# Attention and SoLU MLP on one core: a search for the order of issue that replays each candidate, one DMA moved to another queue, and another order of the first loads

## The chip, the cores and the metric

The kernel runs on one core of one Trainium2 chip. A core has a matrix engine (TensorE, PE in the profile; its weight loads are shown apart as PEld), VectorE (DVE), ScalarE (ACT), GpSimd (POOL) and SyncE (SP), each with its own instruction queue that it works off in order, and 16 DMA engines that they share. "SPq" and "ACTq" in the profile are the queues through which SyncE and ScalarE issue DMAs. The metric is the device time of one execution in microseconds (us); lower is better. The kernel before took 397.25 us in the median of 3 runs (396.76 to 397.73).

## What is computed

Block-sparse attention over 4 batches, 8 heads, 768 positions and 64 channels a head, and then a SoLU MLP over the 3072 tokens of 512 channels (inner width 1024). Each query sees the keys nearer than 16 positions and, for each block of 32 positions, one summary key (the maximum over the block) with one summary value (the mean over the block).

```python
k_sum = k.reshape(B, H, nb, block, D).max(axis=3)
v_sum = v.reshape(B, H, nb, block, D).mean(axis=3)
scores_l = where(|i - j| < 16, scale * q @ k.T, -1e9)
scores_s = scale * einsum('bhsd,bhnd->bhsn', q, k_sum) + log(block)
a = softmax(concat([scores_l, scores_s]))
x = a @ concat([v, v_sum])            # then (B*S, H*D)
h = x @ w_in
solu = h * softmax(h)
out = ((solu - mean) / sqrt(var + 1e-6) * g_ln) @ w_out
```

## The kernel before, in words

**Tiles and stages.** Queries are handled in groups of 256 positions, three groups to a batch, so 12 groups; a group is handled in two halves of four heads. A query tile of 64 positions sees a window of 96 keys and the 24 block maxima, 120 columns in all. For each half group there is a matmul step for the scores (`scores`, line 578; masked on VectorE at line 597, exponentiated on ScalarE at line 605, normalised at lines 610 to 615), a transpose (`values_turn`, line 633) and the product with the values (`values`, line 672), whose result is copied out of the accumulator as a rounded high part (`xh`, line 677) and a rest (`xl`, line 678). The value tile `vt` of a group holds 96 window rows in its partitions and, in partitions 96 to 119, the 24 block means, which a small DMA (`load_v2`, line 541) copies from the tile `vsum`.

The MLP works on 24 tiles of 128 tokens: `first` (line 697: 24 matmuls of 512 columns for both halves, then maxima, exponentials, products and sums on VectorE, ScalarE and GpSimd), `turn` (transpose, and split into a high part and a rest) and `second` (line 775: 24 matmuls, then a scaled copy at line 780 and the store at line 785). The weights come as 64-bit words and are split on the chip into a rounded high part and a rest (`rounded`, lines 359 to 389; `split_w_in`, `split_w_out`), some seven operations a piece of 512 KB, on ScalarE, VectorE and, for some, GpSimd. There are 8 pieces of `w_in` and 8 of `w_out`. All of that splitting falls into the first 100 us.

**Block means.** Batch 0's are summed by matmuls over rows loaded for that purpose (`mean_values_first`, line 459) and land in `vsum`. Batch 1's are summed likewise at line 472, copied to a tile `vs` on ScalarE, and from there four small DMAs on ScalarE's queue (line 485) put them into `vsum`. There is one buffer for `vsum`, so batch 1's may be written only when the last DMA that reads batch 0's has landed; that last one is the third group's `load_v2`. Batches 2 and 3 are summed on GpSimd (`add_rows`, line 501) and one matmul (line 516).

**What sets the order.** The code does not issue instructions as it goes. Each step is recorded by `op` (line 107) with the engines that could do it, a cost on each, what it reads and writes, and a number that is its place in the program (`prio`). Then `Plan.issue` (line 141) works out an order: `due` is the least place of any matrix-engine operation that depends on the step, or for SyncE's DMAs their own place. `order` (line 172) simulates: at each step it takes, over all engines, the operation that could begin first, and among those that could begin at the same time the one with the least `due`; an operation that several engines can do goes to the one where it would end first, with a surcharge. DMAs share one modelled channel (270 GB/s to 6.9 us, 410 after), begin at the earliest 1 us after issue, and land 0.6 us after their bytes until `LATE`, and 2.0 us after them from then on. `issue` tries the program order once and 63 others, in each of which every `due` has a random number with a spread of 3 added; it keeps the order whose last matrix-engine operation ends first in the simulation. Then the instructions are issued in that order, each engine getting its own in turn. The order is fixed when the program is built. On the chip each instruction waits for what it needs, so an engine whose next instruction is not ready stands still, whatever stands behind it.

While it issues, `issue` follows the simulated time of the matrix engine, and where that has nothing to do before 80 us, `keep_up` (line 243) puts in filler matmuls of zeros (line 900) of 0.22 us each.

**First loads.** `LOADS` (line 47) is a string of letters, one for each of the first 20 DMAs of SyncE: k for the keys of one head pair (410 KB), q for half of the first group's queries (262 KB), w for a piece of `w_in` (524 KB), r for rows for the means (524 KB each, 3 of them), v for the first group's values (1049 KB), Q and V for the second group's queries (524 KB) and values (1049 KB). It gives the places from which the search starts.

**The means of a group.** `load_v2(b, g)` (line 538) waits for `vsum` and for `vt`'s own load, since both write `vt`. For batch 0 it is issued by ScalarE, for the others by SyncE; the first group of batch 0 takes its means straight from `vsum` (line 664) and has no such DMA.

## Time and profile before

| what | us |
|---|---|
| median of 3 runs | 397.25 |
| the profiled execution's own time | 397.45 |
| its span, first to last instruction | 395.7 |
| matrix engine busy (PE) | 386.6 |
| weight loads (PEld) | 298.3 |
| VectorE (DVE) | 275.4 |
| ScalarE (ACT) | 248.7 |
| GpSimd (POOL) | 97.9 |
| last matmul ends | 392.65 |
| bytes moved | 49.24 MB |

In the rows of a timeline stand the start, the length, the engine, the line in the kernel, the operation with what it writes and reads, and how many instructions were merged; in brackets, the idle time of the engine just before and what ended it. In groups of instructions stand the busy time in all, the mean duration in ns, and the idle time before them. A row of busy times by stretch gives, for each engine, busy us and the number of instructions, then the granted clock of the matrix engine, the share of time that the DMA engines were busy, and GB/s. In the chain of waits a row is a start, a length and what that time was spent on; "issue" is time in which the engine waited for nothing that the profile shows.

### The profile page before, as it was taken

What the parts mean: (1) busy time and instruction counts of PE and PEld (TensorE: products, weight loads), DVE (VectorE), ACT (ScalarE), POOL (GpSimd) and SP (SyncE); (2) the same over time, 40 slices, a digit from 0 to 9 for tenths busy, and PEclk for the clock granted to TensorE, in tenths of its full rate; (3) what the DMA queues carried; (4) which work ended last, traced back from release to release, by engine and by line L of the source; (5) the groups of instructions that cost most, each with busy time, mean ns of one, the idle gap of its engine ahead of it and who ended that gap; (6) DMA issues with size and microseconds to landing.
All of it is one profiled execution on the core that took longest, in us unless ns stands there. A gap on an engine that the chain in (4) does not pass through costs nothing.

```text
span 395.7 us, 9677 instructions
## 1 busy us (share of the span) xinstructions
PE 386.6 (98%) x3697; PEld 298.3 (75%) x3703; DVE 275.4 (70%) x884; ACT 248.7 (63%) x746; POOL 97.9 (25%) x245
## 2 busy tenths in 40 slices
PE   8999998999999999999999999999999999999996
PEld 3436766677878888878888888878888887878776
DVE  4999998999789866577767657657657654554330
ACT  3889686999798756658558466468466463533411
POOL 4224010416837221236220121221021021101100
PEclk9999999999999999999999999999999999999999
DMA  7999992136277320463330410430310000000011
GB/s 287 411 410 369 409 329 78 56 113 185 70 248 208 113 103 0 141 175 104 123 112 2 150 66 27 156 73 28 108 48 27 2 28 27 16 12 28 27 55 53
DMA packets 14994, 49.24 MB, mean 124 GB/s; under 512 B 1836, under 2 KB 2092, under 8 KB 13412
## 3 DMA queue, kind: packets, MB, share of 16 engines
q1 hardware_dynamic: 11084, 41.89, 30.8%
q10 hardware_dynamic: 3864, 6.74, 4.7%
q8 instruction: 29, 0.48, 0.5%
q14 instruction: 17, 0.14, 0.1%
HBM read 40.11 MB, written 6.29 MB: 117 GB/s over the span
## 4 chain that ended last, share of the span: by engine, by line
PE 85%; DMA 6%; ACT 3%; DVE 2%; issue 1%; ACTq 1%; SPq 1%; DVEq 0%
PE o L775 35%; PE h L697 30%; PE x L672 6%; PE s L578 5%; PE t L633 3%; PE lt L633 3%; DMA st_v<-in_vr 3%; DMA raw<-in_w_in 2%; DMA vt<-vsum 2%; PE vs_ps L459 1%; PE x L900 1%; ACT he L712 1%; DVE he L720 1%; ACT at L281 1%; PE x L664 1%
## 5 line engine op out<-in xcount | busy, mean ns | idle before, releaser
L775 PE MATMUL o<-w,lh 128*128 128x512 f32 (+1 forms) x400 | 128.0, 390 | 0.1
L697 PE MATMUL h<-w,xh 128*128 128x512 f32 x384 | 127.0, 398 | 0.4 <-DVE he L720 0.4
L605 ACT ACTIVATE e<-e,nm 128x120 f32<-128x120 f32 x192 | 73.1, 385 | 25.0 <-DVE nm L597 25.0
L775 PEld LDWEIGHTS o<-w,lh 128*128 128x128 f32 x400 | 74.1, 188 | 18.5 <-issue 2.4
L697 PEld LDWEIGHTS h<-w,xh 128*128 128x128 f32 x384 | 72.1, 188 | 18.9 <-ACT e L605 0.8
L775 PE MATMUL o<-w,ll 128*128 128x512 f32 (+1 forms) x200 | 76.9, 384 | 0.0
L697 PE MATMUL h<-w,xl 128*128 128x512 f32 x192 | 75.6, 394 | 0.0
L707 DVE TENSOR_REDUCE hm<-h 128x1 f32<-128x512 f32 x48 | 32.6, 686 | 42.7 <-PE h L697 42.7
L281 ACT COPY at<-t 120x512 f32<-120x512 f32 x46 | 24.8, 587 | 46.1 <-PE t L633 45.6
L775 PEld LDWEIGHTS o<-w,ll 128*128 128x128 f32 x200 | 37.6, 188 | 6.6
L697 PEld LDWEIGHTS h<-w,xl 128*128 128x128 f32 x192 | 36.1, 188 | 7.5
L597 DVE CUSTOM_DVE_ANT_0 e<-s,mask 128x120 f32<-128x120 f32 x192 | 40.6, 276 | 1.3 <-PE s L578 1.3
L712 ACT ACTIVATE he<-h,hm 128x512 f32<-128x512 f32 x48 | 32.8, 697 | 9.4 <-DVE hm L709 9.4
L605 ACT ACTIVATION_READ_ACCUMULATOR e<-e,nm 128x1 f32 x192 | 36.5, 190 | 0.0
L760 DVE TENSOR_TENSOR ll<-lt,lh 128x512 fp32r<-128x512 f32 x48 | 31.9, 682 | 6.0 <-ACT lh L281 5.8
L739 POOL TENSOR_SCALAR ss<-ss 128x1 f32<-128x1 f32 x24 | 7.1, 297 | 115.0 <-ACT sq L735 114.9
L720 DVE SCALAR_TENSOR_TENSOR he<-h,hz,he 128x512 f32<-128x512 f32 x48 | 34.1, 746 | 0.4
L672 PE MATMUL x<-at,vt 120*64 120x64 f32 (+1 forms) x768 | 28.3, 225 | 1.5 <-ACT at L281 1.5
L672 PEld LDWEIGHTS x<-at,vt 120*64 120x64 f32 (+1 forms) x768 | 24.6, 138 | 6.3 <-ACT at L281 2.8
L288 DVE TENSOR_TENSOR e<-e,z 128x960 f32<-128x960 f32 x23 | 26.6, 1156 | 0.5
L281 ACT CAST lh<-lt 128x512 fp32r<-128x512 f32 x33 | 18.6, 596 | 12.9 <-PE lt L633 10.0
L735 ACT ACTIVATE sq<-he 128x1024 bf16<-128x1024 f32 x24 | 25.2, 1050 | 0.2
(94 smaller groups left out, 499.6 us busy)
## 6 DMA issues: line engine op xcount, KB each, us to landing
vt<-in_v SPq DMA_DIRECT2D x12, 1024.0 KB, 5.4
kraw<-in_k SPq DMA_DIRECT2D x16, 400.0 KB, 9.1
out<-os ACTq DMA_DIRECT2D x23, 256.0 KB, 2.0
qt<-in_q SPq DMA_DIRECT2D x11, 512.0 KB, 5.5
raw<-in_w_in SPq DMA_DIRECT2D x8, 512.0 KB, 10.7
raw<-in_w_out SPq DMA_DIRECT2D x8, 512.0 KB, 9.5
st_v<-in_vr SPq DMA_DIRECT2D x6, 512.0 KB, 12.5
st_v<-in_vb SPq DMA_DIRECT2D x8, 384.0 KB, 3.3
```

Of the source, the lines that this page charges most:

```text
L281: by = {act: lambda: nc.scalar.copy(out=to(), in_=of()), dve: lambda: nc.vector.tensor_copy(out=to(), in_=of()), pool: lambda: nc.gpsimd.t ...
L288: by = {dve: lambda: nc.vector.tensor_tensor(out=to(), in0=a(), in1=b(), op=kind), pool: lambda: nc.gpsimd.tensor_tensor(out=to(), in0=a() ...
L597: nc.vector.tensor_tensor_reduce(out=e.ap[:, n, :], in0=sc.ap[:, j, (2 * i + up) * KC:(2 * i + up + 1) * KC], in1=mask[:, mi, :], scale=-S ...
L605: nc.scalar.activation(out=e.ap[:, n, :], in_=e.ap[:, n, :], func=AF.Exp, bias=nm.ap[:, n:n + 1], scale=-1.0, accum_out=z.ap[:, n:n + 1])
L672: nc.tensor.matmul(xp()[j * D:(j + 1) * D, i, qs], vs.ap[:k, u, cs], at.ap[:k, u % 2, n[j] + u // 2, :], start=not apart, stop=not apart o ...
L697: nc.tensor.matmul(hp.ap, a.ap[:, c, ts], w.ap[:, i], start=(c == 0 and n == 0), stop=(c == NKC - 1 and n == 2))
L707: op(dve, 0.6, lambda i=i, hp=hp: nc.vector.tensor_reduce(out=nms.ap[:, i:i + 1], in_=hp.ap, op=ALU.max, axis=AX.X, negate=True), r=[hp], ...
L712: op(act, 0.71, lambda i=i, hp=hp: nc.scalar.activation(out=part(i), in_=hp.ap, func=AF.Exp, bias=nm.ap, accum_out=zs.ap[:, i:i + 1]), r=[ ...
L720: op(dve, 0.67, lambda i=i, hp=hp: nc.vector.scalar_tensor_tensor(out=part(i), in0=hp.ap, scalar=zs.ap[:, 0:1], in1=part(i), op0=ALU.mult, ...
L735: op(act, 1.13, lambda: nc.scalar.activation(out=sq.ap, in_=e.ap, func=AF.Square, accum_out=ss.ap), r=[e], w=[sq, ss])
L760: op(dve, 0.6, lambda part=part, r=r: nc.vector.tensor_tensor(out=part(lo), in0=tp.ap[:, r], in1=part(hi).bitcast(F32), op=ALU.subtract), ...
L775: nc.tensor.matmul(o.ap[:, cols], a.ap[:, f, :], w.ap[:, i, cols], start=(f == 0 and n == 0), stop=(f == NFC - 1 and n == 2))
```

## The change

Four things are changed. The search tries 800 orders instead of 64: the program order, 15 in which every `due` gets a random number with a spread of 10 added, and then 784 in each of which about 2% of the steps get another such number on top of the best found so far. A new function `replay` scores an order: it keeps the order and the choice of engines, and goes through it again with durations of all engines but the matrix engine between 1.2% shorter and 4.8% longer, and with landings after `LATE` later by a random time of 1.5 us in the mean. An order's score is the sum over six such replays of the end of the last matrix-engine operation plus half the mean of all their ends; the lowest score is kept. In the simulation, `LATE` is 30 instead of 50 us, and landings after it take 2.5 instead of 2.0 us. The third group's means of batch 0 are issued by SyncE instead of ScalarE. The string of the first loads is another.

```diff
-LOADS = "wwkwqkkkqwwwrrrwwvQV"
+LOADS = "wwkqkkkwqwwrwrrvQwwV"
...
-    LATE = 50.0
+    LATE = 30.0
...
-    TRIES, NOISE = 64, 3.0
+    TRIES, NOISE = 800, 10.0
+    FIRST, FEW = 16, 0.02
+    PLAYS, JITTER, LAND = 6, 0.06, 1.5
...
-        due, best = [o.due for o in self.ops], None
-        for seed in range(self.TRIES):
-            noise = random.Random(seed)
-            for o, x in zip(self.ops, due):
-                o.due = x + (noise.gauss(0.0, self.NOISE) if seed else 0.0)
+        due, best, rnd = [o.due for o in self.ops], None, random.Random(0)
+        for i in range(self.TRIES):
+
+            noise = [x + (rnd.gauss(0.0, self.NOISE) if i < self.FIRST or rnd.random() < self.FEW else 0.0) * (i > 0)
+                     for x in (best[3] if i >= self.FIRST else [0.0] * len(due))]
+            for o, x, n in zip(self.ops, due, noise):
+                o.due = x + n
             order = self.order()
             if order:
-                end = max(o.end for o in order if "pe" in o.can)
-                if best is None or end < best[0]:
-                    best = end, order, [(o.start, o.end, o.engine, o.cost, o.fn) for o in self.ops]
-        _, order, kept = best
+                kept = [(o.start, o.end, o.engine, o.cost, o.fn) for o in self.ops]
+                end = sum(self.replay(order, random.Random(k)) for k in range(self.PLAYS))
+                if best is None or end <= best[0]:
+                    best = end, order, kept, noise
+        _, order, kept, _ = best
...
+    def replay(self, order, rnd):
+
+        free, end, held, dma, last, total, n = {}, {}, 0.0, 0.0, 0.0, 0.0, 0
+        for o in order:
+            e = o.engine
+            t = max([free.get(e, self.START)] + [end[d] + (0.0 if d.engine == e == "pe" else self.SYNC) for d in o.deps])
+            x = o.can[e][0] * (1 if e == "pe" else 1.0 + self.JITTER * (rnd.random() - 0.2))
+            other = free.get("pool", 0.0) if e == "dve" and o.port else held if e == "pool" else 0.0
+            x = t + x * (2 if e == "pe" and t < self.COLD else 1) + max(other - t, 0.0)
+            free[e] = end[o] = x
+            if e == "dve" and o.port:
+                held = x
+            if o.nbytes:
+                dma = max(dma, x + 1.0) + o.nbytes / (self.RATE if dma > self.COLD else self.SLOW) * 1e-3
+                end[o] = dma + (0.6 if dma < self.LATE else 2.5) + rnd.expovariate(1.0) * self.LAND * (dma > self.LATE)
+            if e == "pe":
+                last, total, n = max(last, x), total + x, n + 1
+        return last + 0.5 * total / n
...
-                o.end = dma + (0.6 if dma < self.LATE else 2.0)
+                o.end = dma + (0.6 if dma < self.LATE else 2.5)
...
-        e, cost, queue = (sp, 0.43, nc.sync) if b else (act, 0.8, nc.scalar)
+        e, cost, queue = (sp, 0.43, nc.sync) if b or g > 1 else (act, 0.8, nc.scalar)
```

## Prediction, made before the changed kernel was run

> **What bounds the kernel now.** I read the page first, then the busy times by stretch, the matmul engine's groups, its timeline, the chain that ended last, and the timelines of ScalarE, VectorE and the load queue.
>
> ```profile
> span 395.7 us, 9677 instructions
> PE 386.6 (98%) x3697; PEld 298.3 (75%) x3703; DVE 275.4 (70%) x884; ACT 248.7 (63%) x746; POOL 97.9 (25%) x245
> ```
>
> PE is busy for 98% of the span, but an average over stages says little. The stretches (us from the span's start; then the length and the busy time of PE, PEld, DVE, ACT and POOL; then clock, DMA share and GB/s) separate the stages:
>
> ```profile
> 0.00:10.00 10.00, 8.55 (x57) 3.60 (x58) 4.45 (x8) 3.75 (x5) 4.21 (x18) 1.00 0.79 288
> 10.00:20.00 10.00, 8.90 (x121) 4.90 (x123) 9.86 (x46) 8.61 (x27) 2.43 (x2) 1.00 1.03 412
> 20.00:38.30 18.30, 17.46 (x205) 8.40 (x207) 18.27 (x59) 16.14 (x57) 6.58 (x15) 1.00 1.03 394
> 38.30:60.00 21.70, 21.70 (x210) 15.72 (x207) 21.00 (x58) 16.85 (x52) 1.64 (x2) 1.00 1.02 363
> 60.00:70.00 10.00, 8.99 (x120) 6.77 (x118) 8.27 (x19) 6.74 (x14) 1.21 (x3) 1.00 0.25 66
> 70.00:97.00 27.00, 25.48 (x270) 18.39 (x268) 26.75 (x97) 26.22 (x76) 11.42 (x26) 1.00 0.36 113
> 97.00:392.65 295.65, 295.56 (x2726) 240.50 (x2724) 186.78 (x603) 169.93 (x520) 70.37 (x181) 1.00 0.24 79
> 392.65:395.70 3.05, 0.00 (x0) 0.00 (x0) 0.00 (x0) 0.47 (x1) 0.00 (x0) 0.87 0.13 43
> ```
>
> From 97.00 to 392.65 us PE lacks 295.65 - 295.56 = 0.09 us, and line 900, the filler, has no matmul there: a new order of the same work can gain nothing in that stretch, only lose. The last 3.05 us are the final copy and store. So everything is decided before 97 us. There VectorE is the full engine (10 to 60 us: 50.00 - 49.13 = 0.87 us idle), DMA runs at 363 to 412 GB/s until 60 us, and PE's busy time contains fillers:
>
> ```profile
> L900 PE MATMUL vs_ps<-zero 128*128 128x512 bf16 x50 | 13.9, 433 | 1.6 <-DVE zero L303 1.2 <-issue 0.3
> L900 PE MATMUL x<-zero 128*128 128x512 bf16 x21 | 5.4, 381 | 0.2 <-issue 0.2
> L900 PE MATMUL h<-zero 128*128 128x512 bf16 x6 | 1.5, 379 | 0.2 <-issue 0.2
> ```
>
> That is 20.8 us of matmuls that compute nothing, put where the plan itself saw PE waiting. Where they and the idle times lie is told by PE's timeline:
>
> ```profile
> 11.16 3.84 PE L900 MATMUL vs_ps<-zero 128*128 128x512 bf16 x16
> 20.52 1.88 PE L459 MATMUL vs_ps<-st_v,sel 128*24 128x512 f32 x4 [0.90 <-DMA st_v<-in_vr]
> 38.32 0.50 PE L697 MATMUL h<-w,xh 128*128 128x512 f32 x1
> 66.42 1.15 PE L672 MATMUL x<-at,vt 120*64 120x64 f32 x32 [1.01 <-ACT at L281]
> 70.45 0.50 PE L697 MATMUL h<-w,xh 128*128 128x512 f32 x1 [0.36 <-DVE he L720]
> 73.32 0.39 PE L900 MATMUL x<-zero 128*128 128x512 bf16 x1
> 78.24 1.46 PE L900 MATMUL x<-zero 128*128 128x512 bf16 x6
> 80.27 0.82 PE L900 MATMUL x<-zero 128*128 128x512 bf16 x3
> 93.48 1.04 PE L672 MATMUL x<-at,vt 120*64 120x64 f32 x28 [0.53 <-ACT at L281]
> ```
>
> So there are two places to win: the start, until the first MLP matmul at 38.32 us, and the stretch from 60 to 97 us. Between them PE is full.
>
> The second place begins with a wait that the chain of waits shows (start, length, what), and that ScalarE's timeline shows from its own side:
>
> ```profile
> 53.50 6.18 DMA vt<-vsum
> 59.69 1.35 issue
> 61.04 0.72 ACTq L485
> ```
>
> ```profile
> 52.99 1.08 ACT L281 COPY at<-t 120x512 f32<-120x512 f32 x2
> 53.50 0.81 ACTq L541 DMA_DIRECT2D vt<-vsum  x1
> 53.93 0.72 ACT L712 ACTIVATE he<-h,hm 128x512 f32<-128x512 f32 x1
> 61.89 0.84 ACT L281 COPY kw<-kraw 128x768 f32<-128x768 f32 x1 [2.20 <-issue]
> 61.90 2.13 ACTq L485 DMA_DIRECT2D vsum<-vs  x3
> 64.08 0.72 ACT L400 ACTIVATE w<-cv,g_sb 128x512 fp32r<-128x512 f32 x1 [1.35 <-issue]
> ```
>
> The DMA at 53.50 is the third group's means. It reads the one vsum buffer, which the four small DMAs of line 485 overwrite with batch 1's means. They stand in ScalarE's queue and wait for its landing at 59.69; all that is queued behind them there waits too: 2.20 + 1.35 = 3.55 us of idle ScalarE, then PE's 1.01 us at 66.42. VectorE stands still with it:
>
> ```profile
> 64.83 0.75 DVE L402 SCALAR_TENSOR_TENSOR w<-cv,g_sb,w 128x512 fp32r<-128x512 f32 x1 [1.14 <-ACT w L400]
> 66.98 1.29 DVE L379 SCALAR_TENSOR_TENSOR cv<-cv 128x512 int32<-128x512 int32 x2 [0.59 <-ACT cv L374]
> ```
>
> **Part 1: the third group's means move from ScalarE's to SyncE's queue.** Removed from ScalarE: one issue of 0.81 us. It lies under the two copies of 52.99 to 54.07, and the next activation starts at 53.93, so it costs nothing now and its removal gains nothing; with that cover gone it would be 0.81. Added to SyncE: one issue, which waits for the vsum copy and for the group's v load. Behind it in SyncE's queue stand later loads of v, q and keys. The DMAs of line 485 must still wait for its landing. The landing does not move by itself; what can move is where the plan puts those four DMAs, since a transfer's landing is now reckoned 2.5 us behind it from 30 us on (before: 0.6 us until 50 us and 2.0 after that), and the replays add a random delay. The plan of before let ScalarE sit 59.69 to 61.04 for this; an order that expects a late landing puts ScalarE work there. Of the 3.55 us, the four issues themselves remain. PE's 1.01 us at 66.42 goes or stays: ends 0 and -1.0; I take **-1.0**, because the wait behind it is 1.35 us and lies wholly in the part that reordering can fill.
>
> The Trainium skill, "DMA: Bandwidth & Descriptors", section "Issuing engines are not separate DMA queues", speaks against a gain from the move: DMAs of all issuers share the same 16 DMA engines, and a second issuer saves only sequencer time. By that rule alone this part would be 0 instead of -1.0, and the forecast 1.0 higher; the 0.81 us of issue, hidden here, agrees with it. I keep -1.0 since I take it from the reordering, not from the queue.
>
> **Part 2: what follows in 70 to 97 us.** The stretch lacks 27.00 - 25.48 = 1.52 us on PE and holds 0.39 + 1.46 + 0.82 = 2.67 us of fillers, 4.19 us together. VectorE is busy 26.75 of 27.00 there and ScalarE 26.22, so PE waits for work that comes late through them. What they lost just before is 10.00 - 8.27 = 1.73 us of VectorE in 60 to 70 us, of which 1.14 + 0.59 are the two rows above. Closed in full it moves VectorE's later work up by 1.73; not closed, 0. I take about half, **-0.8**, because the second half of ScalarE's hole is its own four issues, and they stay.
>
> **Part 3: the start.** Five rows of the load queue's timeline before:
>
> ```profile
> 4.89 1.17 SPq L430 DMA_DIRECT2D kraw<-in_k  x2
> 6.54 0.98 SPq L356 DMA_DIRECT2D raw<-in_w_in  x2
> 8.18 0.33 SPq L529 DMA_DIRECT2D qt<-in_q  x1
> 9.56 1.62 SPq L447 DMA_DIRECT2D st_v<-in_vr  x2
> 14.16 0.33 SPq L447 DMA_DIRECT2D st_v<-in_vr  x1
> ```
>
> The whole order there was w k q q k w w w k k w w Q r r w v r w V: the old string, shaken by the search. By the sizes in the code (w 0.524 MB, k 0.410, half q 0.262, Q and r 0.524, v 1.049) the last key stands at 4.26 MB and the third r at 8.98 MB. In the new string they stand at 2.95 and 6.88 MB, the last w at 9.50 MB in both. At 412 GB/s the keys would land 1.31 / 0.412 = 3.2 us sooner, where PE now spends 3.84 us in fillers waiting for them, and the means' rows 5.1 us sooner. But the new search shakes more (noise 10 instead of 3 on a scale where one step is one operation), so the string is no promise. And VectorE is full: to start the MLP x us sooner, its work has to be done sooner or elsewhere. It has 0.87 us idle from 10 to 60; ScalarE has 50.00 - 41.60 = 8.40, so copies that both can do may move. The gain lies between 0 and 3.2 us, not below unless the w are pushed back, and the last w is not; I take **-1.5**, the middle of 0 and 3.2 rounded, somewhat above the 0.87 that VectorE has free. The moved SyncE issue plays no part here.
>
> **Part 4: the steady stretch.** All priorities are drawn anew, so the order after 97 us changes too. Gain 0; a new wait would be of the kind in the rows above, 0.36 to 1.01 us. PE has work queued there and every order tried is replayed with durations of the other engines 1.2% shorter to 4.8% longer (the factor in the new replay), so I take **0**, with +1.0 as the other end.
>
> Sum: -1.0 - 0.8 - 1.5 + 0 = -3.3 us. The profiled execution took 397.45 us (span 395.7 and 1.75 around it): 394.15. The median of the runs is 397.25, 0.2 lower: **394.0 us**. The case's own range runs from -(1.0 + 1.73 + 3.2) = -5.9, 391.3, to 396.4.
>
> **Rivals.** *A: no change* (397.3). The search finds orders that only look better: each of its 800 orders is scored on six replays whose random draws fall differently on each order, so the lowest score is partly luck, and VectorE's work before 97 us is the same in sum. For it: 0.87 us idle VectorE from 10 to 60 us. Against it: the 1.73 us hole and the 20.8 us of fillers are there to be had.
>
> *B: slower through SyncE's queue.* The means now stand behind key and v loads in one queue, and their landing sets when ScalarE's four DMAs may go. Loads of that queue landed so late after issue (median us, last):
>
> ```profile
> kraw<-in_k SPq DMA_DIRECT2D x16, 400.0 KB, 9.1
> st_v<-in_vr SPq DMA_DIRECT2D x6, 512.0 KB, 12.5
> ```
>
> Against 6.18 us from ScalarE's queue, 9.1 to 12.5 means 2.9 to 6.3 us more, 4.6 in the middle, and ScalarE stands that much longer if the four DMAs are planned no later. Parts 1 and 2 then turn from -1.8 to about +3.8 (4.6 less the 0.8 that stays); with -1.5 from the start the sum is +2.3: 399.6. It decides once the landing comes more than some 2.3 us later than now, that is over 8.5 us after issue. Against it: DMA share falls to 0.25 after 60 us, and the replays allow for late landings. The Trainium skill, same page, section "Queues, rings and completion order", has each DMA engine take turns between the issuers' queues packet by packet, while within one queue's ring it goes in order; by that rule a DMA moved into the busier queue loses its turn. No row of before shows this DMA issued from SyncE under load.
>
> *C: more than forecast.* If the reordering also takes all 4.19 us from 70 to 97 us, parts 1 to 3 come to 1.0 + 4.19 + 3.2 = 8.4 at the most; the middle between 5.9 and 8.4 is 7.15: 390.1. Against it stands VectorE's 26.75 of 27.00.
>
> **How the numbers follow.** About 0.2%, 0.8 us, is what a measurement of this kernel can tell from no change. Chances: forecast 0.64, A 0.13, B 0.14, C 0.09. Faster: 0.64 + 0.09 = 0.73; same 0.13; slower 0.14. The range 391.0 to 399.5 leaves out most of C and the upper half of B, 0.15, and some 0.05 of the forecast's ends. Forecast and C, both faster, hold most of the chance.
>
> **What would show it.** Right: the first line 697 matmul starts before 38.3, near 36.8; the 3.84 us of fillers shrink; ScalarE has no 2.20 us hole before line 485's DMAs; fillers and idle PE in 60 to 97 us come to about 5.2 - 1.8 = 3.4 us; from 97 us to the last matmul PE lacks under 0.2 us. Wrong: the same fillers in other places with a first line 697 matmul at 38 us or later (A); the third group's means landing over 8.5 us after issue with ScalarE or PE waiting behind (B); idle PE of 1 us or more after 97 us (part 4).

## The result: 0.57% slower, and the profile after

The changed kernel took 399.63 us in the median of 8 runs (398.51 to 400.08), the kernel before 397.25 (396.76 to 397.73), now in the median of 8 runs too. The ratio is 1.0057, with a 95% interval of 1.0043 to 1.0070. The forecast was 394.0. The profiled execution of the changed kernel took 400.08 us, 2.63 more than the one of before (397.45).

The page of the changed kernel, span and busy times:

```profile
span 398.4 us, 9681 instructions
PE 388.8 (98%) x3699; PEld 296.5 (74%) x3699; DVE 264.4 (66%) x863; ACT 256.6 (64%) x758; POOL 108.5 (27%) x254
```

The matrix engine (PE) computes the same and is busy 2.2 us longer; part of that is matmuls that each take longer, as will be seen. The busy times by stretch (start and end, length, then PE, PEld, DVE, ACT, POOL, granted clock, DMA share, GB/s), from the second stretch on:

```profile
10.00:20.00 10.00, 7.31 (x120) 3.94 (x120) 8.25 (x42) 7.20 (x28) 4.28 (x5) 1.00 1.01 401
20.00:38.30 18.30, 18.30 (x175) 8.73 (x173) 15.80 (x41) 12.37 (x34) 5.30 (x13) 0.91 1.03 399
38.30:60.00 21.70, 21.61 (x234) 14.15 (x236) 20.59 (x69) 21.00 (x67) 3.85 (x3) 1.00 0.95 339
60.00:70.00 10.00, 10.00 (x98) 7.34 (x94) 9.92 (x23) 8.61 (x25) 1.79 (x1) 1.00 0.34 112
70.00:97.00 27.00, 26.35 (x314) 19.51 (x304) 26.40 (x97) 26.86 (x76) 12.63 (x26) 1.00 0.38 116
97.00:395.28 298.28, 296.45 (x2723) 239.07 (x2721) 178.39 (x589) 175.49 (x530) 74.97 (x189) 1.00 0.23 78
```

The last row is the news. From 97 us to the last matmul the work takes 298.28 us where it took 295.65, although PE has three matmuls less to do there (2723 for 2726), and PE lacks 298.28 - 296.45 = 1.83 us, where it lacked 0.09. PE's timeline tells where (the line numbers are 25 higher than before: 722 is the first product, 800 the second, 925 the filler):

```profile
19.87 3.52 PE L484 MATMUL vs_ps<-st_v,sel 128*24 128x512 f32 x4 [2.04 <-DMA st_v<-in_vr]
35.36 0.50 PE L722 MATMUL h<-w,xh 128*128 128x512 f32 x1
46.05 3.63 PE L925 MATMUL x<-zero 128*128 128x512 bf16 x16
57.96 0.82 PE L925 MATMUL t<-zero 128*128 128x512 bf16 x3
74.78 0.82 PE L925 MATMUL x<-zero 128*128 128x512 bf16 x3
80.28 0.60 PE L925 MATMUL x<-zero 128*128 128x512 bf16 x2
82.24 0.61 PE L925 MATMUL x<-zero 128*128 128x512 bf16 x2
121.31 0.68 PE L658 MATMUL t<-ident,e 64*120 64x64 f32 x16 [0.42 <-POOL e L314]
346.42 0.50 PE L722 MATMUL h<-w,xl 128*128 128x512 f32 x1 [0.78 <-DVE xl L703]
374.12 0.50 PE L800 MATMUL o<-w,ll 128*128 128x512 f32 x1 [0.23 <-DVE ll L785]
```

Three things are to be read off. The first MLP matmul starts at 35.36 instead of 38.32 us, but PE then runs out of work: 3.63 us of fillers at 46.05 and 0.82 at 57.96, in a stretch that held neither filler nor idle time before. From 60 to 97 us there is less of both. And three waits stand after 97 us, where there was practically none. ScalarE's timeline at the place of the moved DMA:

```profile
61.60 0.57 ACT L508 COPY vs<-vs_ps 128x512 f32<-128x512 f32 x1
62.20 2.13 ACTq L510 DMA_DIRECT2D vsum<-vs  x3
64.38 0.72 ACT L425 ACTIVATE w<-cv,g_sb 128x512 fp32r<-128x512 f32 x1 [1.38 <-DMA vsum<-vs]
```

The 2.20 us hole ahead of the four small DMAs (line 510 now) is gone; the second half of the hole, 1.38 us, is there as before, since it is the issues themselves.

One further difference stands in no wait. A block is the 24 matmuls of a tile's second product. In the trace of before, first and last matmul of two blocks that follow one another:

```profile
194.82 0.50 PE L775 MATMUL o<-w,lh 128*128 128x512 f32 x1
200.17 0.39 PE L775 MATMUL o<-w,lh 128*128 128x512 f32 x1
209.26 0.50 PE L775 MATMUL o<-w,lh 128*128 128x512 f32 x1
214.69 0.39 PE L775 MATMUL o<-w,lh 128*128 128x512 f32 x1
```

That is 5.35 us and 5.43 us from first to last: the blocks alternate. In the changed kernel such a block takes the longer time:

```profile
194.73 0.50 PE L800 MATMUL o<-w,lh 128*128 128x512 f32 x1
200.17 0.39 PE L800 MATMUL o<-w,lh 128*128 128x512 f32 x1
```

5.44 us. Over the second product the mean from start to start inside the blocks, waits and the first step of a block left out, went from 230.4 to 232.5 ns, so 576 x 2.1 ns = 1.2 us. The first product goes a little the other way: its blocks take 5.37 or 5.27 us before and 5.37 or 5.23 after, the mean went from 231.6 to 231.1 ns, and 576 x 0.5 ns = 0.3 us. Together that is 0.9 us. (The expectations of the first two runs below reckon with the second product alone, and with 1.4 us from 230.1 and 232.6 ns.) Nothing in the code of these matmuls was changed. What did change is where their operands lie: each buffer gets its address in on-chip memory when it is first used while the instructions are issued, so another order moves the buffers.

### The profile page after: what moved, and what is told of

It reads as the page before. It is cut to its first block, busy times and chain, and to the rows that moved or that the text cites. A ratio compares the mean times of both kernels' runs of the same rounds, so it can differ in the third digit from the quotient of the medians.

```text
span 398.4 us, 9681 instructions
## 1 busy us (share of the span) xinstructions
PE 388.8 (98%) x3699; PEld 296.5 (74%) x3699; DVE 264.4 (66%) x863; ACT 256.6 (64%) x758; POOL 108.5 (27%) x254
## 5 line engine op out<-in xcount | busy, mean ns | idle before, releaser
L800 PE MATMUL o<-w,lh 128*128 128x512 f32 (+1 forms) x400 | 131.3, 391 | 0.1
L722 PE MATMUL h<-w,xh 128*128 128x512 f32 x384 | 130.3, 399 | 0.7 <-DVE he L745 0.5
L306 ACT COPY at<-t 120x512 f32<-120x512 f32 x44 | 23.7, 586 | 25.0 <-PE t L658 23.7
L805 ACT ACTIVATE os<-o,y 128x512 f32<-128x512 f32 (+1 forms) x21 | 14.0, 667 | 30.7 <-PE o L800 16.5
L764 POOL TENSOR_SCALAR ss<-ss 128x1 f32<-128x1 f32 x24 | 8.3, 344 | 87.4 <-ACT sq L760 87.2
L753 POOL TENSOR_SCALAR he<-he,nmu 128x512 f32<-128x512 f32 x12 | 12.3, 1029 | 66.1 <-DVE nmu L748 66.1
L306 ACT CAST lh<-lt 128x512 fp32r<-128x512 f32 x39 | 21.7, 601 | 7.5 <-PE lt L658 5.8
```

Source lines behind the costliest of these rows:

```text
L306: by = {act: lambda: nc.scalar.copy(out=to(), in_=of()), dve: lambda: nc.vector.tensor_copy(out=to(), in_=of()), pool: lambda: nc.gpsimd.t ...
L722: nc.tensor.matmul(hp.ap, a.ap[:, c, ts], w.ap[:, i], start=(c == 0 and n == 0), stop=(c == NKC - 1 and n == 2))
L753: op(pool, 0.62, lambda sl=sl: nc.gpsimd.tensor_scalar(out=e.ap[:, sl], in0=e.ap[:, sl], scalar1=nmu.ap, scalar2=1.0, op0=ALU.add, op1=ALU ...
L800: nc.tensor.matmul(o.ap[:, cols], a.ap[:, f, :], w.ap[:, i, cols], start=(f == 0 and n == 0), stop=(f == NFC - 1 and n == 2))
L805: op(act, 0.1 + 0.46 * k, lambda o=o, os=os, cols=cols: nc.scalar.activation(out=os.ap[:, cols], in_=o.ap[:, cols], func=AF.Copy, scale=y.ap),
```

## The experiments

Of all but one of these kernels the search was taken out, and its result written out: the order, the engines, and the order in which buffers get their addresses. Both can then be set apart from each other. No kernel leaves out any of the computation.

```diff
-        due, best, rnd = ...            # the search
+        for w in ORDER.split(): ...     # step, engine, start and end as the search found them
+        for slot in TOUCH.split():
+            self.first[slot].ap         # gives each buffer its address, in this order
```

**Order apart from places, start apart from the rest.** Four kernels on one chip, where the kernel before took 396.82 us.

```diff
 e1:  ORDER of after,   TOUCH of before
 e2:  ORDER of before,  TOUCH of after
 e3:  ORDER of after up to the first PE step planned at 100 us, then the rest in before's;  TOUCH of before
 e4:  ORDER of before up to there, then the rest in after's;  TOUCH of before
```

> The new order of issue, written out, with every buffer at the address it had in the kernel before (buffers get their addresses in the order in which they are first used, so the change moved them). Theory 'places': the 576 matmuls of the second product start 232.6 ns apart in the new kernel and 230.1 in the old because their operands lie elsewhere; with the old places about 576 x 2.5 ns = 1.4 us comes back: 398.2. Theory 'waits': the loss after 100 us lies in matmul waits that the new order opens (1.8 us of idle PE there against 0.1); places change nothing: 399.6. Theory 'queue' (the prediction's rival B): also 399.6.

> The old order, written out, with every buffer at the address it has in the new kernel. Theory 'places': 1.4 us slower than before, 398.6 to 398.7, with the second product's matmuls some 232.5 ns apart. Theories 'waits' and 'queue': 397.25, as before.

> The new order until PE's work of 100 us, then the old order for all that is left, old places. The means' DMA on SyncE is in the new part. Theories 'waits' and 'places' together: the start's gain of some 0.7 us is kept and nothing is lost after it: 396.5. Theory 'queue': the loss comes with the new start: 399 or more.

> The old order until PE's work of 100 us, then the new one, old places, the means' DMA on ScalarE. Theory 'waits': the new rest's 1.8 us of waits come with it: 399.0. Theory 'queue': 397.25, since the DMA is back on ScalarE.

| kernel | us | ratio to before (95%) |
|---|---|---|
| e1, new order | 398.70 | 1.0042 (1.0030 to 1.0054) |
| e2, new places | 397.91 | 1.0021 (1.0012 to 1.0030) |
| e3, new start | 395.89 | 0.9973 (0.9963 to 0.9984) |
| e4, new rest | 400.31 | 1.0083 (1.0070 to 1.0096) |

The new start is worth 0.27%, 0.9 us. The new rest costs 0.69% behind the new start (e1 against e3) and 0.83% behind the old one (e4). The new places cost 0.21% with the old order; with the new one 1.0057 against 1.0042, 0.15%, whose intervals overlap. -0.27 + 0.69 + 0.15 = +0.57: the change makes a gain before 100 us and loses three times as much by the new rest and the places. The busy times of e1 from 97 us to its last matmul:

```profile
97.00:393.15 296.15, 294.25 (x2716) 238.03 (x2714) 176.47 (x584) 173.75 (x521) 72.96 (x186) 1.00 0.24 79
```

and of e3, with the old order in that stretch:

```profile
97.00:391.46 294.46, 294.37 (x2721) 239.52 (x2719) 184.75 (x600) 169.23 (x519) 71.43 (x183) 1.00 0.24 79
```

e1 lacks 296.15 - 294.25 = 1.90 us, e3 0.09: 1.8 us of the difference are PE's waits. The stretch is only 1.7 us longer, but e1 comes to it with 5 matmuls of 0.23 us fewer to do (2716 for 2721), since its profiled execution, 397.98, was its fastest and e3's, 396.31, is above its median. Behind 97 us e1 thus loses 1.7 + 1.2 = 2.9 us, which is what the medians say (2.8). The 1.1 us that are not waits stand in PE's busy time: it is the same within 0.12 us for 5 matmuls fewer. Which of the matmuls take longer there was not settled.

**The queue alone.** The order of before, and only the third group's means issued by SyncE, which is rival B put on the chip.

```diff
-        e, cost, queue = (sp, 0.43, nc.sync) if b else (act, 0.8, nc.scalar)
+        e, cost, queue = (sp, 0.43, nc.sync) if b or g > 1 else (act, 0.8, nc.scalar)
```

> The old order and places, with only the third group's means issued by SyncE at the same place in the order. Theory 'queue': ScalarE's four DMAs wait longer for it, 2 us slower or more, 399.5. Theories 'waits' and 'places': nothing, within 0.5 us of 397.25, since the landing stays where it was and ScalarE's issue of 0.8 us lay under its copies.

397.02 us against 397.20, ratio 0.9996 (0.9981 to 1.0010): no difference. SyncE's queue in that kernel, at the DMA:

```profile
55.28 0.97 SPq L707 DMA_DIRECT2D vt<-vsum  x1
```

and ScalarE behind it:

```profile
60.60 0.84 ACT L448 COPY kw<-kraw 128x768 f32<-128x768 f32 x1 [0.75 <-ACT z L776]
62.75 0.72 ACT L567 ACTIVATE w<-cv,g_sb 128x512 fp32r<-128x512 f32 x1 [1.31 <-DMA vsum<-vs]
```

SyncE issues the DMA at 55.28 us, 1.78 later than ScalarE did, and still ScalarE's holes are 0.75 and 1.31 us, shorter than 2.20 and 1.35: nothing waits longer for the landing. The first of the four small DMAs begins at 59.77 us, so the means had landed 4.5 us after their issue at the latest, where rival B needed over 8.5. Rival B is false. Nor is the short hole the queue's doing: in the profiled executions of the old order with the DMA on ScalarE, the first of the four begins anywhere from 59.98 (h1) to 61.45 us (g3), and PE's wait at 66 us is anything from none (h1) to 1.01 us (before). So the size of this hole differs between executions of one order, with the queue unchanged. The Trainium skill, "DMA: Bandwidth & Descriptors", section "Issuing engines are not separate DMA queues", has it that all issuers' DMAs share the same engines and a second issuer saves only the time of issuing; the ratio 0.9996 agrees.

**The gap at 18 us, and the waits.** In the trace of after, PE idles 2.04 us before the means' matmuls, which then take 3.52 us for four instead of 1.88, at a granted clock of 0.91 in the stretch. e1, with the same order, has the idle time too, but not the slow matmuls behind it:

```profile
19.90 1.88 PE L626 MATMUL vs_ps<-st_v,sel 128*24 128x512 f32 x4 [2.45 <-DMA st_v<-in_vr]
```

So the drop of the clock comes in some executions and not in others. e5 is the changed kernel with nine fillers ahead of these matmuls; e6 is the changed kernel with the producers of four waits moved up in the written order.

```diff
 e5:
+                if o is self.ops[32]:               # the first of the means' matmuls
+                    for _ in range(9):
+                        self.keep_up(at, done)
 e6, in ORDER:
+ the rest xl of one tile (step 1464) ahead of a copy of lh (1459) on VectorE
+ an exponential's product (515) from GpSimd to VectorE
+ the copies of lh of tile 21 (1560, 1562) ahead of the squares of tile 23 (1537)
+ 976 ahead of 977: the two products of tile 13 swapped
```

> The new order and places, with nine more filler matmuls ahead of the first means matmul, where PE sits idle for 2.04 us at 17.8 us because the plan reckons with an earlier landing. Theory 'clock': the four means matmuls took 3.52 us there (1.88 before) at a granted clock of 0.91 in 20 to 38 us, and the first copy that follows is later by that; filled, they take 1.88 and up to 1.6 us comes back in those executions in which it happened: median 398.6, and a narrower spread. Rival 'slack': what hangs on these matmuls waits for VectorE anyway; 399.6.

> The new order and places with five operations moved by hand: the last group's xl subtraction ahead of a weightless copy on VectorE (345 us), one product of exponentials from GpSimd to VectorE (119 us), the last tile's two rounded copies ahead of its squares on ScalarE (371 us), two products of tile 13 swapped on VectorE (226 us). Theory 'waits': PE's waits of 0.78, 0.42, 0.23 and 0.13 us go, and what goes with them: 1.6 us sooner, 398.0. Rival: each wait turns up at the next operation, 399.6.

e5 took 398.74 us against 397.20, ratio 1.0041 (1.0029 to 1.0053). In its PE timeline the gap is closed:

```profile
14.81 4.70 PE L1073 MATMUL vs_ps<-zero 128*128 128x512 bf16 x21 [0.16 <-issue]
19.66 1.88 PE L631 MATMUL vs_ps<-st_v,sel 128*24 128x512 f32 x4 [0.15 <-DMA st_v<-in_vr]
44.21 3.63 PE L1073 MATMUL x<-zero 128*128 128x512 bf16 x15
80.48 0.61 PE L1073 MATMUL x<-zero 128*128 128x512 bf16 x2
```

The four matmuls are back at 1.88 us, 1.64 less, and PE keeps that: the fillers of 46.05 us stand at 44.21, those of 82.24 at 80.48. The profiled execution is 1.28 us shorter (398.80 against 400.08). Between the ratios it is 1.0057 - 1.0041 = 0.16%, some 0.6 us, with intervals that overlap, which fits a drop that only some executions of after have. The granted clocks of the 8 executions of after say so too: the three with a mean of 1.000 took 398.51 to 398.89 us, the five with 0.999 or 0.996 took 399.49 to 400.08; the five of e5 all have 1.000, at 398.59 to 399.22. So the drop is some 0.6 to 0.8 us of the median's 2.4. The gap explains why after's profiled execution is its slowest of 8; it does not explain the whole loss, since e5 is still slower than before by 0.41%, 1.6 us.

The rows at 44 to 46 us say one more thing. Those fillers are put where the plan has PE idle, and run whether the next work is ready or not. In e5 they begin 1.84 us sooner, last as long, and no wait follows them. So what comes behind is not held up by a fixed landing of the loads at the time it has in after. What it waits for is a product on VectorE, as the part on the prediction shows; in e5 that product ends at 47.47 us and PE goes on at 47.53.

e6 took 399.33 us, 1.0056 (1.0043 to 1.0069): no gain. Its waits after 97 us (who waits for whom: us in all, times, longest):

```profile
PE s L744 <- POOL y L904: 0.8, 1, 0.8
PE h L863 <- DVE he L886: 0.8, 1, 0.8
```

The three waits quoted from after's timeline are gone. The swap made its own wait larger (the second row, 0.8 us), and the first row is new. A wait removed by hand came back at another place: mending waits one by one in a written order did not help, as the rival had it.

**Places.** The addresses of the operands were read from the built programs; no view of the profile shows them. The pieces of `w_in` and `w_out` that move through PE, 512 columns a matmul, all start at 96 modulo 256 bytes. The stationary operands `lh` and `ll`, which change by tile, start at 160/96 in even tiles and 96/96 in odd ones before, and at 160/160 and 160/32 after; those of the first product (`xh`, `xl`) at 160/160 and 32/32 before, 160/160 and 96/96 after. In before, the odd tiles, whose `lh` starts where `w` does, have the 5.35 us blocks. The theory called alignment was made of that, and tried in four kernels; before took 397.08 us beside them.

```diff
 g1:  ORDER of before;  TOUCH: lh, ll, xh, xl first, so that all start at 96 modulo 256, like w
 g2:  ORDER of after;   the same TOUCH front
 g3:  as g1, with 128, 32, 64 and 64 unused bytes ahead of four of them: 224; 0; 64; 128, w at 96
 h1:  as g1, with 128 unused bytes ahead of all: the four and w at 224
 g4:  ORDER of e3 (new start, old rest), g1's TOUCH, e5's nine fillers
```

> The old order, with the eight buffers that the MLP's matmuls take as stationary operand (lh, ll, xh, xl, two each) put first in the pool, so that every one begins at 96 bytes past a multiple of 256. Theory 'alignment' (the sharper form of 'places'): in the runs so far blocks whose stationary buffers begin at 96 past a multiple of 256 ran at 227.6 ns a matmul, at 32 past it at 229.2, at 160 past it at 233.4; with all at 96, o's even tiles gain 12 x 24 x 4.9 ns, h's even ones 12 x 24 x 5.9 and its odd ones 12 x 24 x 1.7, together 3.6 us: 393.6. Rival 'distance' (the pace hangs on how far the operands lie apart or on the bank): blocks keep their spread of 227.6 to 233.4 and the time is within 1.5 us of 397.25.

> The new order with the same eight buffers first. Theory 'alignment': o comes from 232.6 to 227.6 ns (2.9 us) and h's even tiles from 233.3 (1.7 us), together 4.6: 395.0, and against the old order with the same places the new one is still 1.2 to 1.5 us slower, by its waits. Rival 'distance': 398 to 400.

> The old order with the eight buffers first, and small pads between them: lh and ll of even tiles begin 224 past a multiple of 256, of odd tiles 0 past it, xh and xl of even groups 64, of odd groups 128. Theory 'alignment': o's and h's blocks show four paces, one for each; if only the place within 128 bytes counts, 224 runs like 96 at 227.6. No forecast of the time beyond 392 to 399. Rival 'distance': the same paces as with all at 96.

> The old order, the eight stationary buffers first, and one pad of 128 bytes ahead of nearly everything, so that the stationary buffers and the weights w, which are the moving operand, both begin 224 past a multiple of 256. Theory 'same place' (both operands at the same distance from a multiple of 256): the pace stays at 226.7 to 227.8 ns and the time at 394.0. Theory 'one good place' (96 past a multiple of 256, whatever the other operand does): 233.3 ns as with stationary buffers at 224, 399.4.

> The new order until PE's work of 100 us, the old one for the rest, nine fillers ahead of the first means matmul, the eight buffers first. If start, rest and places add up: 0.9 us from the start (as measured in the run without these places) and 3.6 from 'alignment': 392.7, faster than both kernels. Rival: the gains overlap, since a faster PE meets the same VectorE before 100 us: 393.5 to 394.

| kernel | us | ratio to before (95%) |
|---|---|---|
| g1, old order, all at 96 | 394.02 | 0.9928 (0.9907 to 0.9948) |
| h1, old order, all at 224 | 394.06 | 0.9932 (0.9910 to 0.9954) |
| g3, old order, all apart from w (2 executions) | 399.38 | 1.0056 (1.0038 to 1.0073) |
| g2, new order, all at 96 | 396.01 | 0.9973 (0.9963 to 0.9983) |
| g4, new start, old rest, all at 96 | 391.98 | 0.9870 (0.9857 to 0.9882) |

(h1 ran in another sitting, beside 397.09 us of before.) Two blocks of the second product that follow one another in g1:

```profile
207.84 0.50 PE L941 MATMUL o<-w,lh 128*128 128x512 f32 x1
213.19 0.39 PE L941 MATMUL o<-w,lh 128*128 128x512 f32 x1
222.12 0.50 PE L941 MATMUL o<-w,lh 128*128 128x512 f32 x1
227.47 0.39 PE L941 MATMUL o<-w,lh 128*128 128x512 f32 x1
```

Both take 5.35 us; the alternation is gone. First and last matmul of a block of the first product, in g3:

```profile
201.44 0.40 PE L866 MATMUL h<-w,xh 128*128 128x512 f32 x1
206.81 0.40 PE L866 MATMUL h<-w,xh 128*128 128x512 f32 x1
```

and in h1:

```profile
198.31 0.39 PE L864 MATMUL h<-w,xh 128*128 128x512 f32 x1
203.52 0.39 PE L864 MATMUL h<-w,xh 128*128 128x512 f32 x1
```

5.37 / 23 = 233.5 ns against 5.21 / 23 = 226.5 ns from start to start. h1 settles what counts: with all operands moved by 128 bytes together the short time stays, so neither of the two addresses is good by itself; both operands have to have the same one. g3's even tiles, at 224 against 96, show that 128 bytes apart does not count as the same. The order loses on its own as well: g2 is slower than g1 by 1.99 us with these operands at the same places.

This also gives the size of the places' share. In e2, the old order with the new places, the second product's blocks all take the longer time (232.5 ns from start to start, 1.2 us), but those of the first product whose operands moved to 96/96 take 5.22 to 5.25 us instead of 5.27 (over all of the first product 230.7 ns instead of 231.6, -0.5 us). The 0.7 us that remain agree with the 0.21%, 0.8 us, of its median.

g4 puts together what was worth something: the new start, the old rest, equal places and the filled gap. At 391.98 us it beats the kernel before by 1.3% and the changed kernel by 1.9%.

**Is the new score at fault, or the draw?** The search is a random one, and the changed kernel is one draw of it. e8 is the changed kernel with another seed and its search left in; the others have their orders written out and g1's places, so that 394.0 us is what the order of before gives there.

```diff
 e8:  after, random.Random(0) -> random.Random(1)
 h2:  before's search, random.Random(seed) -> random.Random(seed + 64);  g1's TOUCH front
 h3:  after's search, random.Random(2);  g1's TOUCH front
 h4:  after's search, only the steps of the first 460 places shaken;  g1's TOUCH front
```

> The new kernel with the search's random numbers begun from 1 instead of 0: another order out of the same search. Theory 'draw': the score does not see PE's small waits and the places, so the chip's time scatters between draws: anywhere from 396 to 400.5, with other waits in other places. Theory 'bias' (something in the new rules makes every order slow): 399 to 400.5 with waits after 100 us of the same 1.7 us or more.

> The old search with 63 other draws (random numbers 65 to 127 instead of 1 to 63), its order written out, the eight stationary buffers first. Compared with the old order so placed, 394.0. Theory 'draw': the old search, too, lands anywhere, 393 to 398, with one or more waits after 100 us. Theory 'spread' (the small spread of 3 keeps the steady stretch near the program's order): 393.5 to 395, under 0.3 us of waits after 100 us.

> The new search with its random numbers begun from 2, its order written out, the eight stationary buffers first. Compared with the new order so placed, 396.0. Theory 'spread' (a spread of 10 shakes the steady stretch, where nothing can be won): waits of 1.5 us or more after 100 us, 396 to 404. Theory 'draw': as likely 393 to 396.

> The new search, with random numbers added only to the first 460 steps of the program, those whose matmuls come before 100 us; its order written out, the eight stationary buffers first. Theory 'spread': waits after 100 us under 0.3 us; 392 to 394, at or under the old order so placed. Rival: the program's own order has waits there too, or the new rules lose in the start: over 394.5.

| kernel | us | ratio to before (95%) |
|---|---|---|
| e8, new search, seed 1, no equal places | 406.96 | 1.0241 (1.0209 to 1.0272) |
| h2, old search, 63 other draws | 397.65 | 1.0023 (1.0003 to 1.0042) |
| h3, new search, seed 2 | 401.27 | 1.0108 (1.0080 to 1.0136) |
| h4, new search, start only | 397.68 | 1.0008 (0.9992 to 1.0024) |

The waits of e8 after 97 us, the three largest:

```profile
PE h L722 <- DVE xl L703: 1.7, 1, 1.7
PE s L603 <- DVE at L307: 1.1, 2, 0.5
PE vs_ps L541 <- DVE hz L743: 1.0, 1, 1.0
```

They are of after's kind, at other places, and larger. In all PE lacks 5.28 us there:

```profile
97.00:402.01 305.01, 299.73 (x2728) 242.27 (x2728) 179.78 (x592) 178.85 (x530) 67.62 (x180) 0.99 0.24 77
```

Some of e8's time is the clock again: its one execution with a mean granted clock of 1.000 took 404.00 us, the others, at 0.996 to 0.986, 405.33 to 408.87. h3 loses most before: the stretch from 38.3 to 60 us of h3, in which PE was full before,

```profile
38.30:60.00 21.70, 19.92 (x201) 13.53 (x203) 20.17 (x58) 15.94 (x54) 5.13 (x5) 0.92 0.91 357
```

lacks 1.78 us of PE at a granted clock of 0.92. And h4, where the rest was not shaken by its own draws, still lacks 1.12 us after 97:

```profile
97.00:392.92 295.92, 294.80 (x2786) 241.82 (x2786) 189.43 (x622) 174.40 (x532) 79.19 (x193) 1.00 0.24 80
```

But that is not its main loss. The five kernels with equal places, side by side: the busy time that PE still has ahead of it at 97 us, what it lacks behind, and what the plan that is written out gives as the end of the last PE step:

| kernel | PE work left at 97 us | PE lacks after 97 us | planned end | measured median |
|---|---|---|---|---|
| g1, old search (before's order) | 291.95 | 0.14 | 395.02 | 394.02 |
| h2, old search | 294.00 | 1.22 | 394.91 | 397.65 |
| g2, new search (after's order) | 291.93 | 2.39 | 393.74 | 396.01 |
| h3, new search | 298.35 | 0.97 | 399.03 | 401.27 |
| h4, new search, start only | 294.80 | 1.12 | 395.73 | 397.68 |

g2 is no worse than g1 at 97 us; what it loses, it loses by waits behind. h2, h3 and h4 lose more before it: 2.1, 6.4 and 2.9 us of work are left over, against 0.8 to 1.1 us of added waits. In h4 that is the part that was shaken.

With equal places the old search's other draws are 3.6 us slower than its order in the kernel before (397.65 against 394.02), and the new search's draws lie at 396.0, 401.3 and, shaking less, 397.7. The theory that the wider shaking does the harm (spread) would have had h4 back near 394 and h2 too; both miss. What the runs show is that the time scatters over several microseconds from draw to draw, in the old search as well, and that the order in the kernel before was a good draw: among the five it is the only one whose measured time lies below its planned end, by 1.00 us, where the others lie 1.95 to 2.74 us above theirs (the two searches reckon landings differently, so compare plans within one search first). The old search keeps the order whose plan ends first, and by that h2, with 394.91, stands 0.11 us ahead of the order of before; the chip has it 3.6 us behind. The three plans of the new search do stand in the chip's order (393.74, 395.73 and 399.03 against 396.01, 397.68 and 401.27): h3 is slow because its search ended at a poor plan, and the 1.28 us by which after's plan is ahead of before's are what the chip does not bear out. What the replays made of these orders is not known here. Two old and four new draws don't tell whether one search is better on average; that stays open.

## Why the prediction was wrong, step by step

**Parts 1 and 2 (-1.8) held, a little more than forecast.** ScalarE's first hole went, the second stayed, as written. Fillers and idle PE from 60 to 97 us fell from 1.01 + 1.52 + 2.67 = 5.20 us to 0.65 + 0.82 + 0.60 + 0.61 = 2.68 us, so -2.5. It came from the order and not from the queue, as part 1 argued: the queue alone is worth nothing in the medians (e7). But up to 1.0 us of it may be the execution: with the old order, too, PE's wait at 66 us is absent in some traces (h1).

**Part 3 (-1.5) took the wrong thing for the gain.** The first MLP matmul came 2.96 us earlier, twice what was forecast, and that in an execution that had lost 1.64 us to the clock just before. But some 1.0 us of it is work put off: of two sets of 32 score matmuls that ran ahead of it, one now runs behind it (at 40.65 us). And 3.63 + 0.82 us of fillers and 0.09 us of idle time follow, where PE was full before. The large piece stands in for a wait for VectorE. The matmuls behind it write the accumulator bank that VectorE reads for its first product `he`. That product before, the same after, and the matmul behind the fillers:

```profile
47.82 0.75 DVE L720 SCALAR_TENSOR_TENSOR he<-h,hz,he 128x512 f32<-128x512 f32 x1
48.57 0.75 DVE L745 SCALAR_TENSOR_TENSOR he<-h,hz,he 128x512 f32<-128x512 f32 x1
49.38 0.54 PE L722 MATMUL h<-w,xh 128*128 128x512 f32 x1
```

The product ends at 49.32 us and PE goes on at 49.38; in e1, e3, e5, g2 and g4, which have the same start, the distance is 0.06 to 0.07 us as well. So the first MLP matmul is 2.96 us earlier, and the product that its successors need is 0.75 us later. From 40.06 to 53.51 us VectorE has no idle time of more than 0.12 us. The 55th matmul of the first product, with all the same work done ahead of it, then begins at 60.73 us instead of 58.13: near 60 us PE is 2.6 us behind instead of 1.5 ahead. The step that failed is the one that booked an earlier start as time saved without asking what the engines behind it allow in the next 25 us. The part itself named the bound, VectorE, and went above it: VectorE does get room, 50.00 - 44.64 = 5.36 us of idle time from 10 to 60 us where it had 0.87, but not where the earlier start needs it. The 2.5 us saved from 60 to 97 us bring most of that back, and something that no row shows the rest: at 97 us PE has 3 matmuls of 0.23 us fewer left than before (2723 for 2726). So the first 97 us brought -0.7 us in the profiled execution, against -3.3 forecast; the medians have 0.9 for it (e3), and 2.0 with the gap filled (g4 against g1, with the same places).

**Part 4 (0, other end +1.0) is the step that turned the sign.** It said that PE has work queued and that the replays with altered durations would keep the order safe. They did not: the plan of after has no idle time on PE behind 100 us, and the chip has 1.83 us. The largest wait, 0.78 us at 346.42, is made on VectorE, which does this just before:

```profile
344.35 0.69 DVE L307 CAST lh<-lt 128x512 fp32r<-128x512 f32 x1 [1.23 <-ACT lh L306]
345.07 0.69 DVE L785 TENSOR_TENSOR ll<-lt,lh 128x512 fp32r<-128x512 f32 x1
345.68 0.68 DVE L703 TENSOR_TENSOR xl<-x,xh 128x512 fp32r<-128x512 f32 x1
```

VectorE stands 1.23 us for ScalarE's half of a copy whose other half it is to write itself; the plan takes the two halves as independent. `xl`, which PE waits for, is queued behind that. In the chip's order of such halves lies one error of the model; which others there are was not settled. The waits cost 1.83 - 0.09 = 1.74 us in the profiled execution, and the new rest 2.8 us between the medians of e1 and e3, of which 1.8 are waits; the other 1.0 is open. As far as waits go, "a new order can gain nothing there, only lose" was right, and should have been priced at more than 0: the old order's 0.09 us there was a result of its own draw, and nothing carried it over. That PE is full did not mean that its work could not go faster: g1, with the order of before, has 291.95 us of PE work behind 97 us where before had 295.55.

**Not in the prediction at all: the places.** 0.9 us by the matmuls' pace in the profiled executions, 0.15 to 0.21% (0.6 to 0.8 us) by the medians of e1 and e2.

In the terms of the profiled executions: -0.7 + 1.74 + 0.9 = +1.9 us, of +2.63. The remaining 0.7 us has no row. In the terms of the medians: -0.9 for the start (e3), where -3.3 was forecast, +2.8 for the rest (e1 against e3), where 0 was, and +0.6 for the places (after against e1), about the 2.4 us by which the change is slower.

Of the five signs of being right that the prediction names, four came true: the early first MLP matmul, the smaller fillers (1.47 us where 3.84 were), ScalarE's hole, and fillers and idle time from 60 to 97 us (2.68 us where 3.4 was named). The sign of part 3 came true without its gain. The fifth, under 0.2 us lacking after 97 us, did not, and of the signs of being wrong that of part 4, 1 us or more there, did.

**The rivals.** B gave 399.6 and the time came out at 399.63, for another reason: e7 and e3, both with the DMA in SyncE's queue, are not slower. A number that fits shows no mechanism. A was nearest in kind: it said that the scores of the search are partly luck, and the draws bear that out; it did not say that the luck of before could be lost. C did not come: 2.68 of the 5.20 us stayed, and the start gave its gain back.

## What to carry to other kernels

A change that redraws an order by a search is priced as a new draw: look at the scatter of a few other draws of the same search before a difference is put down to the search's rules, and leave alone (write out) the stretch in which the bounding engine is already full. An earlier first matmul is a gain only if the engines that feed the next ones are earlier too. Before two orders are compared, fix the addresses of the buffers, since the order of first use moves them.

## What the runs showed of the hardware

A matmul with 512 moving columns and its own weight load took 226.6 to 228.8 ns from start to start, by the means of uninterrupted blocks without their first step, where stationary and moving operand start at the same offset modulo 256 bytes (g1, and all blocks but one of h1, 229.4), and 232.3 to 234.1 ns in g3, where none do. A stationary operand at 32 with a moving one at 96 gave 229.0 to 229.2 ns in the kernel before, one at 160 gave 233.1 to 233.4. Over this kernel's 1152 such matmuls that is worth 5.4 us between g1 and g3 (394.02 and 399.38). The mechanism is not shown; that "the same offset" counts rather than one certain offset is (h1). The Trainium skill, "TensorE: Matmul & The Clock Gate", section "Wait — 56ns, not 53.3ns?", gives 215.7 ns for back-to-back matmuls of 512 columns on a warm array; no run here came to that, the best block mean is 226.6 ns.
